# Slot sums and gathers of the first experts one item sooner, two decayed keys on GpSimd, the decay flag moved

## The chip, the cores and the metric

The kernel runs on one core of a Trainium2 chip. Four engines compute, each with its own program and in its own order: TensorE (PE in the profile, with its weight loads as PEld), VectorE (DVE), ScalarE (ACT) and GpSimd (POOL). SyncE (SP) issues transfers, and so do ACT and POOL. [...] The metric is the time of one execution on the device in microseconds (us); lower is better.

## The reference

Two stages in float32. The first is a linear attention with a decaying state, for 4 batches, 8 heads, 768 tokens and 48 values a head. The second sends each token to one of 8 experts, a network of two layers (384 to 1024 to 384). A token takes the expert of its largest logit, or, where its local gate is at least 0.5, the expert of the token before it.

```python
for t in range(S):
    kt, vt, rt = k[:, :, t], v[:, :, t], r[:, :, t]
    cur = einsum('bhd,bhe->bhde', u * kt, vt)
    y[:, :, t] = einsum('bhd,bhde->bhe', rt, state + cur)
    state = w * state + einsum('bhd,bhe->bhde', kt, vt)
...
fresh_e = argmax(logits[b, s])
e = fresh_e if s == 0 or local_gate[b, s] < 0.5 else prev_e
h = maximum(x[b, s] @ w1[e], 0.0)
out[b, s] = softmax(logits[b, s])[e] * (h @ w2[e])
```

## The kernel before

**Attention.** The work is cut into 16 items, numbered n: a batch and a pair of heads each. An item's 768 tokens are 6 chunks of 128. `scale` makes three products on POOL: `rw` (r times powers of the decay w), `ke` (k for the state) and `pd` (r times k, for a token's own term). `keys` makes `kw`, k times the inverse powers `inv`, on DVE. On PE, `scores` multiplies `kw` by `rw` into a bank called `pair`; DVE masks it into `am`. `own` multiplies `pd` into `y`, and DVE multiplies `y` by v. `added` sums k and v into the states' steps, DVE scans them into `S` (`states`), and `inside` and `before` add `am` and `S` to `y`. ACT copies `y` out as `xT`, `turn` transposes it, and a finished batch goes to memory as `x_d`. `run` interleaves the items by hand: in round n it does the scores of item n+1, the own terms of item n, and `inside` and `before` of item n-1. Item 15 is last; its two halves are copied as `xT` by ACT and as `end` by DVE (L318, L319).

**Routing.** The tokens are routed in two groups of two batches. For group 0 the steps lie between the rounds from n = 9 on (`g` is 8): experts, runs, counts, ranks, `slots` (a token's place in its expert's table), `columns` and `numbers` (tiles `eqv`, `val`), `places`, `apart` and `same` (the one-hot tile `ohq`). Then `summed` multiplies `val` by `ohq` on PE (L846), ACT copies the sums (`rows`), PE transposes them, and `head` turns them into token numbers (`gid`) on DVE. With these, `gather` has POOL fetch the rows of `x_d` (L1107, tile `xg`) for two early units of 168 tokens, units 0 and 1 (experts 0 and 1 with group 0's tokens). In rounds 14 to 16 `piece` brings unit 0's weights in four parts of 768 KB by SP; a one-element copy into each part holds it back until ACT comes by.

**Experts.** Behind the last item come the gate logits of the last batch (`logits`, 8 matmuls in two groups of four heads; a transpose of their result `lT`; a sum on DVE), the transposes of `xg` and their copies `exT`. Unit 0 then runs over eight blocks m of the hidden width: `hidden` (L1134), and one block behind it `output` (L1221). After block m of unit 0 comes step s = m of `routing`, and after block m of unit 1 step s = 8 + m: the same routing again for group 1. Step 4 holds a long run of small operations on DVE, from `exc` to `order` (L761 to L790). Units 0 and 1 are followed by 8 larger blocks, with matmul savings of Strassen's kind (`eleven`, `seven`).

**The decay flag.** `flag(0)` counts on DVE how many of w's values lie in the range for which the kernel is valid (tile `some`, four operations). `flag(1)` sums that over the partitions with a matmul of `some` and a column of ones on PE (L1698), then DVE makes `over` and `rare` of it. They stand in steps 13 and 14. The matmul writes one of two banks, `tp`, that the transposes of `xg` use in turn. Engines take their work strictly in the order in which this code is written.

Of the kernel before, what the change touches and what calls it, by code (L numbers as in the profile page):

```python
# [20 lines left out]
P = 128  # L21
# [31 lines left out]
VB = NCH * 2 * DH  # L53

# [7 lines left out]
class Attention:  # L62
# [140 lines left out]
    def scale(self, n):  # L203
# [28 lines left out]
    def keys(self, n):  # L232
        nc, t = self.nc, self.items[n]
        t["kw"] = self.two.tile([P, NCH, P], F32, name="kw")
        inv = self.inv[:, t["hp"]]
        for z in (slice(0, NCH),) if n > 2 else (slice(0, C2), slice(C2, NCH)):
            nc.vector.tensor_mul(t["kw"][:, z], t["kT"][:, z], spread(inv, 1, z.stop - z.start))
            if n < 3:
                self.decayed(nc.vector, n, z)
# [18 lines left out]
    def own(self, n, part=None):  # L258
# [3 lines left out]
        if part != 1:  # L262
            t["yy"] = y = None if last else self.py.tile([P, 2, 512], F32, name="y")
            t["y"] = [self.banks("yl")[:, 0] if last else y[:, h] for h in range(2)]
        for p in range(2):
            for h in range(2 if part != 1 else 0):
# [5 lines left out]
        if part == 0:  # L272
            return
# [30 lines left out]
    def before(self, n):  # L304
# [5 lines left out]
        for c, h in [(c, h) for h in range(2) for c in range(1, NCH)] if last else [(c, h) for c in range(1, NCH) for h in range(2)]:  # L310
# [44 lines left out]
    def run(self, router, fetch, heads):  # L355
# [11 lines left out]
        for n in range(M + 1):  # L367
# [37 lines left out]
            if n < M:  # L405
                self.turn(n - 2, pair("tp"))
                if n >= M - 2:
                    fetch(2 * (n - M + 2))
# [4 lines left out]
                if n > 3:  # L413
                    if n not in (g + 3, g + 5):
                        self.added(n)
# [12 lines left out]
            if n + 1 < M:  # L428
                self.scale(n + 1)
            if n == g + 6:  # L430
                router.numbers(0, self.nc.gpsimd)
# [7 lines left out]
            if n == g + 6:  # L439
                router.same(0, 1)  # L440
            if M - 2 <= n < M:
                fetch(2 * (n - M + 2) + 1)
            if n == 6:
                router.cast()
            if n == M:
# [20 lines left out]
            if ahead < M:  # L466
                self.scores(ahead, 0)()
# [1310 lines left out]
```

## Time and profile before

| | |
|---|---|
| three runs | 377.18, 378.99, 380.16 us |
| median | 378.99 us |
| the profiled execution's own time | 379.17 us |
| its span (first to last instruction) | 377.5 us |
| granted TensorE clock, mean over the span | 0.996 |
| chain that ended last | one POOL transfer of 0.97 us, 0.3% of the span |

The span is what the trace covers; the rest of the execution's time lies around it. The profiled execution is 0.18 us above the median. Its chain of waits is cut short behind the last transfer, so it says nothing of what bounds the kernel; that has to be read from the waits of PE and from the order of its work in time. In the rows, numbers after an engine's name are a line of the kernel, and a bracket at the end says how long the engine had stood idle and what released it.

### The profile page before, as it was taken

To read this page: it belongs to the slowest core of one execution; us is meant where nothing else is said; L and a number is where in the kernel's file an instruction comes from. 1 tells how busy PE (TensorE), PEld (TensorE's weight loads), DVE (VectorE), ACT (ScalarE), POOL (GpSimd) and SP (SyncE) were. 2 spreads that over 40 slices of the span, in tenths; PEclk is the share of its full clock that TensorE was granted. 3 is DMA by queue.
4 is the path that set the end of the run, shared out by engine and by line. 5 is a ranking of instruction groups with operands and counts; after the bars stand their busy time and mean duration, and the time that the engine had idled before them with its cause. 6 is when DMAs were issued, how large, how long until landed. Compare 5 with 4: busy or idle time off the path is not lost. (4 is left out here: it accounts for less than half of the span.)

```text
span 377.5 us, 9676 instructions
## 1 busy us (share of the span) xinstructions
PE 363.0 (96%) x3844; PEld 319.6 (85%) x3844; DVE 247.7 (66%) x718; ACT 110.3 (29%) x304; POOL 148.7 (39%) x207
## 2 busy tenths in 40 slices
PE   7899999999989999999999999999999999999992
PEld 6676777786769998999899999999999998989971
DVE  6988778888834835787557656857767767555300
ACT  4132233233532211322332233333243233331210
POOL 7689999786222055212333113313233023021012
PEclk9999999999999999999999999999999999999998
DMA  7999999983669457713352452164165065162011
GB/s 245 417 411 410 407 405 338 370 300 109 196 232 340 160 188 296 299 27 115 140 198 62 147 214 87 49 218 190 38 207 213 22 215 206 21 257 112 2 41 38
DMA packets 17765, 74.93 MB, mean 199 GB/s; under 512 B 2778, under 2 KB 6624, under 8 KB 15408
## 3 DMA queue, kind: packets, MB, share of 16 engines
q1 hardware_dynamic: 10336, 56.89, 40.7%
q0 software_dynamic: 3424, 9.48, 7.4%
q10 hardware_dynamic: 3952, 7.87, 5.7%
q8 instruction: 32, 0.52, 0.6%
q14 instruction: 21, 0.17, 0.1%
HBM read 64.79 MB, written 9.47 MB: 197 GB/s over the span
## 5 line engine op out<-in xcount | busy, mean ns | idle before, releaser
L1333 POOL DMA_INDIRECT out_dram<-yo,sid x27 | 26.6, 985 | 115.5 <-ACT yo L1328 92.0
L1184 PE MATMUL h<-exT,w1t 128*128 128x168 f32 (+4 forms) x240 | 54.9, 327 | 0.0
L1188 DVE TENSOR_TENSOR hT<-h,hs 128x168 f32<-128x168 f32 (+3 forms) x60 | 21.1, 351 | 46.1 <-PE h L1184 29.6
L1107 POOL DMA_INDIRECT xg<-x_d,gid x29 | 31.1, 1072 | 34.1 <-DVE gid L877 15.1
L1184 PEld LDWEIGHTS h<-exT,w1t 128*128 128x128 f32 x240 | 41.6, 190 | 0.3 <-issue 0.3
L1134 PE MATMUL h<-exT,w1t 128*128 128x168 f32 (+2 forms) x192 | 37.2, 333 | 0.5 <-DVE lt L698 0.5
L1253 PE MATMUL y<-factors,sums 128*128 128x192 f32 x168 | 36.8, 326 | 0.0
L293 DVE TENSOR_TENSOR am<-pair,kept 128x768 f32<-128x768 f32 x32 | 30.0, 953 | 8.9 <-PE pair L291 8.4
L217 POOL TENSOR_TENSOR pd<-rk 128x384 f32<-128x384 f32 x32 | 31.5, 1006 | 10.6 <-PE y L268 10.0
L1184 PE MATMUL h<-xs,ws 128*128 128x168 f32 (+4 forms) x144 | 35.3, 327 | 0.0
L1134 PEld LDWEIGHTS h<-exT,w1t 128*128 128x128 f32 x192 | 30.9, 190 | 2.6 <-DVE lt L698 0.6
L1184 PEld LDWEIGHTS h<-xs,ws 128*128 128x128 f32 x144 | 25.5, 190 | 4.3 <-ACT hs L1191 1.2
L1253 PEld LDWEIGHTS y<-factors,sums 128*128 128x128 f32 x168 | 28.9, 190 | 0.2
L291 PE MATMUL pair<-rw,kw 48*64 48x128 f32 (+1 forms) x768 | 23.4, 249 | 1.9 <-issue 1.1
L300 PE MATMUL y<-am,kv 128*64 128x128 f32 x360 | 22.9, 276 | 1.3 <-DVE y L276 1.2
L230 POOL TENSOR_TENSOR rw<-rk,tab 128x384 f32<-128x384 f32 x26 | 23.7, 936 | 0.4 <-DMA rk<-in_rk_dram 0.4
L1121 DVE COPY exT<-tp 128x384 f32<-128x384 f32 (+5 forms) x29 | 13.9, 485 | 14.7 <-PE tp L1120 14.6
L291 PEld LDWEIGHTS pair<-rw,kw 48*64 48x64 f32 x768 | 19.6, 133 | 4.6 <-issue 2.8
L1253 PE MATMUL y<-w2t,hT 128*128 128x192 f32 x96 | 23.0, 328 | 0.0
L213 POOL TENSOR_TENSOR ke<-kv,endT 128x288 f32<-128x288 f32 (+1 forms) x32 | 21.9, 705 | 1.9 <-DMA kv<-in_kv_dram 1.0
L321 ACT COPY xT<-y 128x768 f32<-128x768 f32 x15 | 12.0, 800 | 33.1 <-PE y L313 31.1
L300 PEld LDWEIGHTS y<-am,kv 128*64 128x64 f32 x360 | 19.4, 137 | 2.4 <-DVE y L276 1.7
(298 smaller groups left out, 736.6 us busy)
## 6 DMA issues: line engine op xcount, KB each, us to landing
w1t<-in_w_dram SPq DMA_DIRECT2D x8, 1536.0 KB, 6.9
w2t<-in_w_dram SPq DMA_DIRECT2D x8, 1536.0 KB
rk<-in_rk_dram SPq DMA_DIRECT2D x15, 768.0 KB, 8.4
kv<-in_kv_dram SPq DMA_DIRECT2D x16, 584.0 KB, 7.1
vT<-in_vT_dram SPq DMA_DIRECT2D x16, 384.0 KB
x_d<-x ACTq DMA_DIRECT2D x4, 1152.0 KB
w1t<-in_w_dram SPq DMA_DIRECT2D x2, 768.0 KB
w2t<-in_w_dram SPq DMA_DIRECT2D x2, 768.0 KB
```

The lines of the kernel that those rows point to most:

```text
L213: nc.gpsimd.tensor_mul(t["ke"][:, z], t["k"][:, z], spread(self.endT[:, p, hp], 1, len(range(NCH)[z])))
L217: nc.gpsimd.tensor_mul(t["pd"][:, z], t["rT"][:, z], t["kT"][:, z])
L230: engine.tensor_mul(t["rw"][:, z], t["rT"][:, z], spread(pw, 1, z.stop - z.start))
L291: nc.tensor.matmul(sc[f * DP:(f + 1) * DP, h, i, x:], lhsT=t["kw"][q, c, o * DP:(o + 1) * DP], rhs=t["rw"][q, c, x:], start=True, stop=True)
L293: return lambda: nc.vector.tensor_mul(t["am"][:, g], sc, spread(self.kept[:, g:g + 3], 1, 2))
L300: nc.tensor.matmul(t["y"][h][p * DP:(p + 1) * DP, c2 * P:(c2 + 1) * P], lhsT=t["v"][:, (2 * c + h) * DH:(2 * c + h) * DH + DP], rhs=t["am" ...
L1107: self.nc.gpsimd.indirect_dma_start(out=xg[:n], out_offset=None, in_=self.x_d[:rows], in_offset=bass.IndirectOffsetOnAxis(ap=u["gid"][:n, ...
L1134: nc.tensor.matmul(h[:, :n], lhsT=u["w1"][:, m, kk, :], rhs=u["xT"][:, kk, :], start=(kk == 0), stop=(kk == DK - 1))
L1184: nc.tensor.matmul(out, lhsT=a, rhs=b, start=start and k == 0, stop=stop and k == len(terms) - 1, skip_group_check=True)
L1188: nc.vector.tensor_tensor(out, a, b, op=Alu.add)
L1253: return lambda: nc.tensor.matmul(bank[:, x * half:(x + 1) * half], lhsT=a, rhs=b, start=(j == 0 and x == 0), stop=(j == FK // 2 - 1), ski ...
L1333: self.nc.gpsimd.indirect_dma_start(out=out.rearrange("n (h d) -> (n h) d", h=2) if half else out, out_offset=bass.IndirectOffsetOnAxis(ap ...
```

## The change

Its parts:

- For items 14 and 15 (`LATE`) `kw` is made on POOL instead of DVE, in two halves, between `ke` and `pd`. Since POOL takes its factor from SBUF, ACT copies two heads' pairs of `inv` to a tile `held` in round 6.
- Routing of group 0: `columns`, `places` (now two quarters on DVE) and `same` stand earlier, `numbers` stands ahead of `pd` of item 15, and `summed` moves from between the own terms of item 15 to the end of round 14. `head` and `gather` move to the start of round 15, behind `turn(13)`.
- The fourth part of unit 0's weights is held back by POOL until the rows of the second gather have landed.
- `before` of item 15 takes its two heads in turn, as with the other items, and no longer one after the other.
- Behind the last logits both tiles of `xg` are transposed first, then `lT`, then the last item; ACT copies the second tile, and also one tile of unit 2 in block 5 of unit 1.
- The decay flag moves from steps 13 and 14 to steps 5 and 6, and its matmul now takes `some` as a weight that is repeated over 128 columns.

```diff
-    def scale(self, n):
+    def scale(self, n, ahead=None):
...
         for what in (pd, ke) if n < 3 else (ke, rw, pd) if n == 4 else (rw, ke, pd):
+            if n in LATE and what is pd:
+                self.keys(n, nc.gpsimd)
+                if ahead:
+                    ahead()
             for i in range(2):
                 what(i)
...
-        for c, h in [(c, h) for h in range(2) for c in range(1, NCH)] if last else [(c, h) for c in range(1, NCH) for h in range(2)]:
+        for c, h in [(c, h) for c in range(1, NCH) for h in range(2)]:
...
                 self.turn(n - 2, pair("tp"))
+                if n == g + 6:
+                    router.same(0, 1)
+                if n == g + 7:
+                    router.head(self.pairs[0][:, 1, C2 * P:])
+                    heads()
...
+                self.held = self.late.tile([P, len(LATE), P], F32, name="held")
+                self.nc.scalar.copy(self.held, self.inv[:, HP - len(LATE):])
...
-                self.own(n, 0)
-                router.summed(0, 0)
-                self.own(n, 1)
-                router.copied(0)
+                self.own(n)
                 spare = self.py.tile([P, 2, 512], F32, name="y")
                 self.turn(n - 1, [spare[:, 0], spare[:, 1]])
-                router.head(self.pairs[0][:, 1])
-                heads()
...
             if n == g + 6:
-                router.places(0, 0)
+                self.added(n + 1)
+                router.summed(0, 0)
+                router.copied(0)
...
-        nc.scalar.copy(t[0:1, z.start, 0:1], self.ident[0:1, 0:1])
+        if k == 3:
+            nc.gpsimd.tensor_copy(t[0:1, z.start, 0:1], u["xg"][-1][0:1, 0:1])
+        else:
+            nc.scalar.copy(t[0:1, z.start, 0:1], self.ident[0:1, 0:1])
...
+        if s == 5:
+            self.flag(0)
         if s == 6:
+            self.flag(1, bank("fp"))
             self.fetch(EARLY, self.nc.sync, 1)
...
-        if s == 13:
-            self.flag(0)
-        if s == 14:
-            self.flag(1, bank("fp"))
...
+        for j in range(len(self.units[0]["rows"])):
+            self.turn(0, j, self.nc.scalar.copy if j else None)
+        att.token_logits(B - 1, yb[0])
         att.turn(B * HP - 1, yb[1:])
-        self.turn(0, 0)
-        att.token_logits(B - 1, yb[0])
-        self.turn(0, 1)
...
-                nc.tensor.matmul(fp[:1, :1], lhsT=some, rhs=router.ones[:, 0:1], start=True, stop=True)
+                nc.tensor.matmul(fp[:, :1], lhsT=some.to_broadcast([P, P]), rhs=router.ones[:, 0:1], start=True, stop=True)
```

In the lists that follow, a row is one or more instructions of one engine in program order, with the line of its own version of the kernel, the operation, the tile written and the tiles read.

POOL, items 14 and 15, before: `pd` of item 15 is followed by `val`, and that by the gathers of unit 0.

```order
L213 TENSOR_TENSOR ke<-kv_169,endT 128x3x96
L213 TENSOR_TENSOR ke<-kv_169,endT 128x2x96
L217 TENSOR_TENSOR pd<-rk_159 128x384 x2
L230 TENSOR_TENSOR rw<-rk_160,tab 128x384 x2
L213 TENSOR_TENSOR ke<-kv_165,endT 128x3x96
L213 TENSOR_TENSOR ke<-kv_165,endT 128x2x96
L217 TENSOR_TENSOR pd<-rk_160 128x384 x2
L818 TENSOR_TENSOR val_117<-eqv_116,t_527 128x384
L1107 DMA xg<-x_d,gid_95 128x384
L1107 DMA xg<-x_d,gid_95 40x384
```

The same place on POOL now.

```order
L214 TENSOR_TENSOR ke<-kv_169,endT 128x3x96
L214 TENSOR_TENSOR ke<-kv_169,endT 128x2x96
L245 TENSOR_TENSOR kw<-rk_159,held 128x384 x2
L218 TENSOR_TENSOR pd<-rk_159 128x384 x2
L235 TENSOR_TENSOR rw<-rk_160,tab 128x384 x2
L214 TENSOR_TENSOR ke<-kv_165,endT 128x3x96
L214 TENSOR_TENSOR ke<-kv_165,endT 128x2x96
L245 TENSOR_TENSOR kw<-rk_160,held 128x384 x2
L827 TENSOR_TENSOR val_117<-eqv_116,t_527 128x384
L218 TENSOR_TENSOR pd<-rk_160 128x384 x2
L1118 DMA xg<-x_d,gid_95 128x384
L1118 DMA xg<-x_d,gid_95 40x384
```

Two `kw` have come in ahead of the two `pd`, and `val` has gone ahead of the last one.

PE, from the last item's states to unit 0's first matmul, before (`lT` are the transposed logits, `end` the last head's output, `h` the hidden layer).

```order
L313 MATMUL pair_152<-rw,S 48x128 x5
L313 MATMUL pair_151<-rw,S 48x128 x5
L345 MATMUL y_1963<-xT,wp 32x384 x7
L345 MATMUL y_1963<-end_1895,wp 32x384
L332 MATMUL y_1964<-ident,xT 128x112 x3
L332 MATMUL y_1965<-ident,end_1895 128x112 x3
L1120 MATMUL tp_1938<-ident,xg 128x128 x3
L351 MATMUL y_1963<-ident,lT 128x128 x3
L1120 MATMUL tp_1937<-ident,xg 128x40 x3
L1134 MATMUL h<-exT,w1t 128x168 x6
```

The same place on PE now, from the last of the states' matmuls on.

```order
L318 MATMUL pair_152<-rw,S 48x128
L318 MATMUL pair_151<-rw,S 48x128
L350 MATMUL y_1968<-xT,wp 32x384 x7
L350 MATMUL y_1968<-end_1900,wp 32x384
L1131 MATMUL tp_1943<-ident,xg 128x128 x3
L1131 MATMUL tp_1942<-ident,xg 128x40 x3
L356 MATMUL y_1968<-ident,lT 128x128 x3
L337 MATMUL y_1969<-ident,xT 128x112 x3
L337 MATMUL y_1970<-ident,end_1900 128x112 x3
L1145 MATMUL h<-exT,w1t 128x168 x6
```

The states' matmuls alternate between the two banks, and the transposes of `xg` stand ahead of those of `lT` and of the last item.

PE behind block 6's hidden layer of unit 0, before.

```order
L1134 MATMUL h<-exT,w1t 128x168 x3
L1221 MATMUL y_2027<-hT,w2t 128x168
L1221 MATMUL y_2028<-hT,w2t 128x168
L1221 MATMUL y_2029<-hT,w2t 128x168
L1120 MATMUL tp_1937<-ident,xg 128x128 x3
L1134 MATMUL h<-exT,w1t 128x168 x3
```

The same place on PE now.

```order
L1145 MATMUL h<-exT,w1t 128x168 x3
L1232 MATMUL y_2032<-hT,w2t 128x168
L1232 MATMUL y_2033<-hT,w2t 128x168
L1232 MATMUL y_2034<-hT,w2t 128x168
L1708 MATMUL tp_1942<-r_ones,some 128x1
L1131 MATMUL tp_1943<-ident,xg 128x128 x3
```

The flag's matmul has come in ahead of the transposes of unit 1's first tile.

DVE at the end of step 4, before (`order` is the order of the blocks).

```order
L788 TENSOR_TENSOR num<-of,ief 1x64
L789 TENSOR_REDUCE orderf<-num 1x8
L790 CAST order<-orderf 1x8
L1121 COPY exT<-tp_1937 128x3x128
L1121 COPY exT<-tp_1938 128x3x40
```

The same place on DVE now.

```order
L797 TENSOR_TENSOR num<-of,ief 1x64
L798 TENSOR_REDUCE orderf<-num 1x8
L799 CAST order<-orderf 1x8
L1703 TENSOR_SCALAR ok<-w_t 128x4
L1704 TENSOR_SCALAR ok<-w_t 128x4
L1705 TENSOR_TENSOR ok<-ok 128x4
L1706 TENSOR_REDUCE some<-ok 128x1
L1709 TENSOR_SCALAR over<-tp_1942 1x1
L1710 CAST rare<-over 1x1
L1132 COPY exT<-tp_1943 128x3x128
```

The flag's six operations have come in between the last one of step 4 and the copies of unit 1's tiles.

More of the change, by code (lines that the diff above doesn't have):

```diff
@@ L1111, in gather, with turn @@
             u["xg"].append(xg)
-    def turn(self, i, j):
+    def turn(self, i, j, copy=None):
         nc, u = self.nc, self.units[i]
@@ L1568, in run @@
                 if m >= FK - after and not (following and m == FK - 1):
-                    self.turn(i + 1, m - (FK - after))
+                    self.turn(i + 1, m - (FK - after), self.nc.scalar.copy if following and m == FK - 3 else None)
             if i + 1 == EARLY:
@@ L1682 @@
         att = Attention(tc, st, rk_d, kv_d, vT_d, x_d, w_t, wp_d, kept, ident, lt, router.mp)
-        att.run(router, ex.piece, lambda: ex.gather(0))
+        att.run(router, ex.piece, lambda: (ex.gather(0), ex.piece(3)))
         ex.open(st)
```

52 lines of the change are left out of this document (26 added, 26 removed).

## The prediction

> **What bounds the kernel now.** I read the page's busy times first, then the waits of PE, then PE's program in time around the places that the change touches, and then DVE and POOL at the same times. From the page:
>
> ```profile
> PE 363.0 (96%) x3844; PEld 319.6 (85%) x3844; DVE 247.7 (66%) x718; ACT 110.3 (29%) x304; POOL 148.7 (39%) x207
> ```
>
> PE has work in 363.0 of 377.5 us. Of the 14.5 us left, some 7.4 lie behind its last matmul (370.04, below) and 1.6 ahead of its first (the first row of the next list). So whatever the change can win lies in a few short stalls, or in matmuls that run closer together, and whatever it adds to PE's waits lengthens the run. The waits of PE alone, by who was waited for:
>
> ```profile
> PE pair L151 <- POOL ident masks.py:199: 1.6, 1, 1.6
> PE tp L1120 <- DVE over L1699: 0.7, 1, 0.7
> PE tp L1120 <- DMA xg<-x_d,gid: 0.6, 1, 0.6
> PE h L1134 <- DVE lt L698: 0.5, 1, 0.5
> ```
>
> The other three are what the change is about: the flag, the first gather, and the copies ahead of unit 0's first matmul. Together they are under 2 us, 0.5% of the run. Here is PE's program between the last item and unit 0, in order of time (start, length, matmul records, and idle time before them):
>
> ```profile
> 106.93 1.20 PE L313 MATMUL pair<-rw,S 48*48 48x128 f32 x20
> 108.06 1.49 PE L345 MATMUL y<-xT,wp 128*32 128x384 f32 x14
> 109.23 0.83 PE L345 MATMUL y<-end,wp 128*32 128x384 f32 x2
> 109.99 0.51 PE L332 MATMUL y<-ident,xT 112*128 112x112 f32 x3
> 111.34 0.55 PE L1120 MATMUL tp<-ident,xg 128*128 128x128 f32 x3 [0.56 <-DMA xg<-x_d,gid]
> 111.73 0.49 PE L351 MATMUL y<-ident,lT 128*128 128x128 f32 x3
> 112.15 0.37 PE L1120 MATMUL tp<-ident,xg 40*128 40x40 f32 x3
> 113.02 1.98 PE L1134 MATMUL h<-exT,w1t 128*128 128x168 f32 x12 [0.50 <-DVE lt L698]
> ```
>
> From 106.93 to 113.02 are 6.09 us. The same steps in rounds where nothing waits, and the copy that the last logits wait for:
>
> ```profile
> 97.09 0.79 PE L313 MATMUL y<-rw,S 48*48 48x128 f32 x18
> 97.62 0.28 PE L291 MATMUL pair<-rw,kw 48*64 48x128 f32 x2
> 87.77 1.50 PE L345 MATMUL pair<-xT,wp 128*32 128x384 f32 x16
> 89.20 0.79 PE L332 MATMUL pair<-ident,xT 112*128 112x112 f32 x6
> 108.62 0.56 DVE L319 COPY end<-pair 128x384 f32<-128x384 f32 x1 [2.30 <-PE pair L313]
> ```
>
> **Between the last item and unit 0: 1.8 us gained.** An item that takes its two heads in turn has its states' matmuls through in 97.62 - 97.09 = 0.53, a little more with the two records that lie past it, say 0.63; item 15, one head after the other, takes 108.06 - 106.93 = 1.13. The new order makes it an item like the others: 0.5 gained. Eight logits without a wait take 89.20 - 87.77 = 1.43; here they take 109.99 - 108.06 = 1.93, because the last one starts at 109.23, behind the copy that ends at 109.18. In the new order that copy can still only start when the states are through, but the first four heads' logits (half of 1.43) cover its 0.56 nearly whole: some 0.4 gained. The two stalls of 0.56 and 0.50 are the third part. The gather is issued earlier (next paragraph), so the first should go. For the second, the transposes of `lT` and of the last item now stand between those of `xg` and unit 0; they take about 0.4 and 0.8 and cover both copies, with the short one on ACT behind `lT`. Sum 0.5 + 0.4 + 0.56 + 0.50 = 1.96; I take a gain of 1.8, nearer the upper end, since three of the four parts are read straight from rows and only the cover of the copies is argued. Bounds: 1.06 (the stalls alone) and 2.0. Late next is nothing on PE; ACT comes to the last item's copies and the store of `x_d` about 1 us later against unit 0, but the first gather that reads it starts at 132.88 (row below).
>
> **The sooner sums, and `kw` on POOL: 0.** The matmuls of `summed` stand at 103.84 and move to behind `added`, near 100.2; POOL's first gather starts at 106.45 and would start near 102.9.
>
> ```profile
> 100.42 0.66 PE L249 MATMUL mp<-kv,ke 128*48 128x48 f32 x20
> 103.84 0.86 PE L846 MATMUL mp<-ohq,val 128*32 128x128 f32 x24
> 84.42 1.35 POOL L213 TENSOR_TENSOR ke<-kv,endT 128x288 f32<-128x288 f32 x2
> 88.75 1.76 POOL L230 TENSOR_TENSOR rw<-rk,tab 128x384 f32<-128x384 f32 x2
> 94.66 1.98 POOL L217 TENSOR_TENSOR pd<-rk 128x384 f32<-128x384 f32 x2 [2.85 <-PE y L268]
> 106.45 1.27 POOL L1107 DMA_INDIRECT xg<-x_d,gid  x1 [7.72 <-DVE ex L919]
> 132.88 1.07 POOL L1107 DMA_INDIRECT xg<-x_d,gid  x1 [15.10 <-DVE gid L877]
> 92.33 0.28 PE L291 MATMUL pair<-rw,kw 48*64 48x128 f32 x2
> ```
>
> The first rows arrived 111.34 - 106.45 = 4.9 after the issue; the same from 102.9 gives 107.8, and PE wants them at 109.99 less the 0.9 gained ahead of them, 109.1. The tile `kw` is a product with a repeated factor like `rw`, so 1.8 to 2.0 for both halves. POOL ends `ke` of item 14 at 85.77 and makes `kw` by 87.8; PE's scores want it at 92.33. Then `pd`, `rw` and `ke` of item 15 run to about 92.8, `kw` of item 15 to 94.8, and its scores come at 97.62 (row above). POOL was idle for 2.85 ahead of the last `pd`, and the own terms that read it come at about 104. So POOL's 4 extra us lie beside other work with 2.8 us to spare, and DVE's 1.9 us of relief help nobody, since no wait above names `kw`. If POOL were slower by half, the cover would still hold. The one copy of `held` on ACT (0.4 to 0.5), the ACT copies of `exT`, and the fourth weight part, which is now held until about 108 and read by PE near 121, I cost at nothing for the same kind of reason: ACT is busy 29% of the time, and no PE wait above names it there.
>
> **The old flag: 0.85 gained.** The flag's matmul stands where the `xg` transposes need its bank:
>
> ```profile
> 142.63 0.19 PE L1698 MATMUL tp<-r_ones,some 128*1 128x1 f32 x2
> 143.50 0.87 PE L1120 MATMUL tp<-ident,xg 128*128 128x128 f32 x6 [0.69 <-DVE over L1699]
> ```
>
> From 142.63 to 143.50 are 0.87, matmul and stall together; without them 0.85 is saved (bounds 0.69 and 0.87).
>
> **The new flag: 3.9 lost.** Its matmul now stands on PE just ahead of the transposes at 125.38, and what it waits for, `some`, is made on DVE behind the whole of step 4:
>
> ```profile
> 124.52 1.02 PE L1221 MATMUL y<-hT,w2t 128*128 128x168 f32 x6
> 125.38 0.49 PE L1120 MATMUL tp<-ident,xg 128*128 128x128 f32 x3
> 122.18 0.37 DVE L761 TENSOR_TENSOR_SCAN exc<-seg,ext 128x104 f32<-128x104 f32 x1 [1.31 <-ACT ext L760]
> 128.35 0.16 DVE L790 CAST order<-orderf 1x8 int32<-1x8 f32 x1
> 128.43 0.73 DVE L1121 COPY exT<-tp 128x384 f32<-128x384 f32 x2
> 140.90 0.16 DVE L1693 TENSOR_SCALAR ok<-w_t 128x4 f32<-128x4 f32 x1
> 141.36 0.16 DVE L1696 TENSOR_REDUCE some<-ok 128x1 f32<-128x4 f32 x1
> 122.18:128.51 6.33, 6.33 (x66) 5.95 (x64) 5.81 (x19) 1.00 (x4) 0.00 (x0) 1.00 0.50 192
> ```
>
> The last row is a stretch: PE busy 6.33 of it, PEld 5.95, DVE 5.81 in 19 operations. DVE works through step 4 from 122.18 to 128.51 almost without a gap; it starts when the counts of the same step leave PE, so the block moves with PE and stays as late against it. Before the change the `exT` copies simply queued behind it and PE had other matmuls. Now the four operations of `flag(0)` follow at 128.43 and take 141.52 - 140.90 = 0.62: `some` is there at 129.05. PE loads it as a weight and runs the matmul (0.19), and is at the transposes at about 129.3 instead of 125.38: 3.9 lost. Behind the waiting matmul stand all of PE's later work, and with it the hidden layer, ACT and the next step of the routing; nothing of that can overtake. Bounds: 3.4, if DVE's gaps (6.33 - 5.81 = 0.5) closed, and 4.2 with slower hand-overs. No later stall of PE's list can take this up, since those left are under 1 us.
>
> **The sum.** -1.8 - 0.85 + 3.9 = +1.25 on the profiled execution's own 379.17, which gives 380.4; on the median of 378.99, which stands 0.18 lower, 380.2, and I say 380.3. With all bounds at one end: +0.5 (3.4 - 2.0 - 0.87) to +2.45 (4.2 - 1.06 - 0.69), so 379.5 to 381.4.
>
> **Rivals.** First, PE's clock falls in the new gap. What this trace shows of it is the end of the run (PE busy is the second number, its clock the third from the right):
>
> ```profile
> 367.64:370.05 2.41, 2.40 (x30) 1.84 (x26) 0.31 (x1) 0.00 (x0) 0.97 (x1) 1.00 0.16 57
> 371.10:374.40 3.30, 0.00 (x0) 0.00 (x0) 0.00 (x0) 0.00 (x0) 0.66 (x1) 1.00 0.15 36
> 374.50:377.40 2.90, 0.00 (x0) 0.00 (x0) 0.00 (x0) 0.00 (x0) 0.00 (x0) 0.50 0.03 8
> ```
>
> The last matmul ends at 370.04, the clock is still whole at 374.40 and half from 374.50: it took 4.4 us of idling, and the new gap is 3.6 to 3.9 (from 125.54, where the outputs end, or from 125.38). So by the row the clock stays. But one drop doesn't fix the point, and if the gap is enough in a run, the matmuls behind it run at half speed for a stretch, by my estimate about as long as the gap: half of 3.5, or 1.7, is lost, giving 382.0. If a second such stretch passes before the clock returns, 3.4 is lost, giving 383.7, slower by 1.2%; it decides from about 5 us at half clock on. [...] I give the first price 0.15 and the second 0.06.
>
> Second, the gap isn't there or is short, because `some` is ready near 125.4: then the change does what its flag edit can do at best, and the sum is -1.8 - 0.85, or 376.3. Against it stand DVE's order and the block of step 4 ahead of it. It would need the block to end 3 us sooner. 0.08.
>
> Third, POOL is late after all: `kw` for item 15 or the last `pd` misses its matmul, or the gather lands after 109.1. Each tenth of lateness beyond the 2.8 (or 1.3) spare shows one for one; I price it at the stalls that come back, 1.06, and half a us more, 380.3 + 1.06 + 0.5 = 381.9. POOL's rows of 1.7 to 2.0 for such pairs speak against it. 0.09.
>
> **How the numbers follow.** The forecast, a stall on the flag with the clock kept, has 0.62, with 379.5 to 381.4 as its own range. The three runs before spread over 377.2 to 380.2, 0.4% either way, so I widen: 378.7 at the low end. The high end, 382.9, takes in one stretch of half clock and a late POOL. A measurement of this kernel can tell about 1% from no change, 3.8 us: faster would need less than 375.2, below even the second rival, so 0.02. Slower needs over 382.8: the second price of the clock rival, and a tail of the others, 0.09. Within 1%: 0.89.
>
> **What would show it.** In the profile after: PE idle for about 3.6 us ahead of the one-column matmul of `some`, released by DVE, and no idle time ahead of the first `xg` transposes or unit 0's first matmul; the 20 states' matmuls of item 15 in about 0.6; from the first of them to unit 0 about 4.3 instead of 6.09; no PE wait on POOL's `kw`; the granted clock whole behind the gap. The forecast is wrong if that gap is under 2 us, or if the clock falls.

## The result, and the profile after

The changed kernel takes 387.08 us in the median of six runs (385.4 to 388.63), the kernel before 378.24 beside it (377.18 to 380.16). The ratio is 1.023, with a 95% interval of 1.020 to 1.025: 2.3% slower, where 380.3 was forecast with 382.9 as the upper end. The profiled execution is one of the quicker ones, 385.40 us with a span of 383.6, which is 6.23 above the profiled execution before. PE's busy time in the page after:

```profile
PE 364.2 (95%) x3844; PEld 320.5 (84%) x3844; DVE 246.5 (64%) x715; ACT 111.2 (29%) x306; POOL 152.5 (40%) x212
```

PE has as many matmuls as before and is busy 1.2 us longer, so some of them ran slower. The other 5 us are idle time. PE's waits after (who waited, for whom, us in total, times, longest) name it:

```profile
PE tp L1708 <- DVE some L1706: 3.5, 1, 3.5
PE tp L1131 <- DMA xg<-x_d,gid: 2.5, 1, 2.5
...
PE pair L864 <- ACT x L339: 0.8, 1, 0.8
...
PE y L1232 <- ACT hT L1148: 0.4, 1, 0.4
```

The first is the forecast gap. The second is a wait for the rows of unit 3, which the prediction didn't have at all; the 0.6 that the list before had under the same name were for unit 0's rows. The last two are small and new. PE's program in time around the last item (start, length, records, idle time before and its releaser):

```profile
101.59 0.33 PE L864 MATMUL pair<-ident,rows 128*128 128x128 f32 x1 [0.79 <-ACT x L339]
...
107.29 0.90 PE L318 MATMUL pair<-rw,S 48*48 48x128 f32 x20
...
111.39 1.89 PE L1145 MATMUL h<-exT,w1t 128*128 128x168 f32 x12
113.72 1.09 PE L1232 MATMUL y<-hT,w2t 128*128 128x168 f32 x6 [0.45 <-ACT hT L1148]
```

From 107.29 to 111.39 are 4.10 where there were 6.09, and neither the transposes of the gathered tiles nor unit 0's first matmul wait any more. But PE comes to 107.29 0.36 later than before (106.93), and unit 0's first output now waits. PE's program from unit 0's end to unit 3's first rows:

```profile
123.48 1.02 PE L1232 MATMUL y<-hT,w2t 128*128 128x168 f32 x6
128.03 0.38 PE L1708 MATMUL tp<-r_ones,some 128*128 128x1 f32 x2 [3.53 <-DVE some L1706]
128.28 0.53 PE L1131 MATMUL tp<-ident,xg 128*128 128x128 f32 x3
...
130.10 1.89 PE L1232 MATMUL y<-hT,w2t 128*128 128x168 f32 x6
...
133.16 1.12 PE L1232 MATMUL y<-hT,w2t 128*128 128x168 f32 x6
...
147.83 1.12 PE L1145 MATMUL h<-exT,w1t 128*128 128x168 f32 x6
...
157.75 0.55 PE L1131 MATMUL tp<-ident,xg 128*128 128x128 f32 x3 [2.47 <-DMA xg<-x_d,gid]
158.13 0.74 PE L1232 MATMUL y<-hT,w2t 128*128 128x168 f32 x4
```

Six outputs take 1.02 at 123.48 and 1.89 at 130.10. The stretches after say why; in each row the PEclk, third from the right, is the mean granted clock:

```profile
123.50:128.00 4.50, 1.00 (x8) 0.74 (x6) 4.17 (x15) 0.31 (x1) 0.00 (x0) 1.00 0.39 161
128.00:129.00 1.00, 0.97 (x8) 0.97 (x9) 0.45 (x3) 0.00 (x0) 0.00 (x0) 0.93 0.00 0
129.00:130.00 1.00, 1.00 (x5) 1.00 (x5) 0.39 (x1) 0.00 (x0) 0.00 (x0) 0.50 0.00 0
...
132.00:134.00 2.00, 2.00 (x33) 1.74 (x34) 0.28 (x1) 0.52 (x2) 0.00 (x0) 0.93 0.90 369
```

A mean of 0.93 over 128 to 129 puts the fall at 128.86 (0.14 us at half), and 0.93 over 132 to 134 the return at 132.27: 3.4 us at half clock, all of them with work. The same instruction in both programs, by its start, gives the account:

| PE instruction | before | after | after - before | what lies between |
|---|---|---|---|---|
| unit 0's first matmul | 113.02 | 111.39 | -1.63 | transition -1.99, 0.36 late into it |
| unit 0's first output | 114.83 | 113.72 | -1.11 | wait of 0.45 |
| unit 0's last but one output | 124.52 | 123.48 | -1.04 | |
| transposes behind the flag | 125.38 | 128.28 | +2.90 | the gap: +3.94 |
| second output behind the flag | 128.61 | 133.16 | +4.55 | half clock: +1.65 |
| unit 1's last hidden block | 144.30 | 147.83 | +3.53 | old flag: -1.02 |
| output behind unit 3's first rows | 151.92 | 158.13 | +6.21 | wait for rows: +2.68 |

After that nothing moves any more; the execution is 6.23 longer. Between these two executions, three terms made the difference to the forecast of +1.25: the clock, a gather that comes late, and -1.04 ahead of the flag where -1.8 was forecast.

Even the -1.04 is more than the change earned. In the profile before, PE stood still for 0.84 in the scores of item 13, which the change leaves as they are:

```profile
85.72 0.21 PE L291 MATMUL pair<-rw,kw 48*64 48x64 f32 x1 [0.84 <-issue]
```

The experiments below have three more profiles with the attention part as it was (flag_only, before_some_early, before_held). None of them has this wait, and they come to unit 0's last but one output at 123.20 to 123.31. Four more with the part as changed (flag_back, some_early, w1_held, filled_gap) come to it at 124.31 to 125.17. So the pair of the table sets a late execution of the old kernel against an early one of the new.

The median lies 1.7 above the profiled execution. Three of the six runs had a mean granted clock of 0.985 to 0.986, where the profiled one had 0.993. A stretch of 3.4 us at half lowers the mean over the run by 0.0044, and the half clock behind the last matmul, 3.0 us long in the profile before (374.47 to 377.5), counts in it too. The profile of flag_only (run 2) shows what 0.985 can be: 6.8 us at half inside the run and 4.5 at its end (380.00 to 384.5), against 3.4 and 2.15 in the changed kernel's. By this estimate the three runs had one stretch more, which is about the 1.7.

### The profile page after: what moved, and what is told of

Same layout as the page of the kernel before. It is cut to its first block, busy times and chain, and to the rows that moved or that the text cites. A ratio compares the mean times of both kernels' runs of the same rounds, so it can differ in the third digit from the quotient of the medians.

```text
span 383.6 us, 9679 instructions
## 1 busy us (share of the span) xinstructions
PE 364.2 (95%) x3844; PEld 320.5 (84%) x3844; DVE 246.5 (64%) x715; ACT 111.2 (29%) x306; POOL 152.5 (40%) x212
```

## The experiments

Theories. **Flag**: the flag's gap and what follows from it cost everything, and without it the rest of the change gains 1.8. **Attention**: the moved sums and gathers also cost something. **Clock**: a part of the loss is half clock behind the gap. **Overtaken gather**: the load of unit 3's first weights (`w1`, 1.5 MB) goes out before the issue of unit 3's first gather has ended, and its bytes delay the rows. **Keys**: `kw` on POOL costs. Each run has its own times of the kernel before, whose medians lie between 378.24 and 378.66; ratios are against those, with 95% intervals.

| kernel | median us | ratio [95%] | PE's wait for unit 3's rows, profiled | gap at the flag |
|---|---|---|---|---|
| changed kernel | 387.08 | 1.023 [1.020, 1.025] | 2.47 | 3.53 |
| 1 flag_back | 379.66 | 1.002 [0.999, 1.005] | 1.46 | none |
| 2 flag_only | 386.63 | 1.022 [1.016, 1.028] | 2.20 | 3.54 |
| 3 some_early | 383.28 | 1.013 [1.007, 1.018] | 2.52 | none |
| 4 before_some_early | 380.21 | 1.005 [1.002, 1.009] | 2.61 | none |
| 5 w1_held | 378.27 | 1.000 [0.997, 1.004] | none | none |
| 6 before_held | 377.35 | 0.998 [0.995, 1.000] | none | none |
| 7 filled_gap | 383.09 | 1.011 [1.007, 1.016] | 0.93 | filled |
| 8 kw_back | 381.07 | 1.007 [1.004, 1.010] | 0.89 | none |
| 9 held_kw_back | 378.50 | 1.000 [0.998, 1.002] | none | none |
| 10 third_first | 378.35 | 0.998 [0.995, 1.001] | none | none |
| 11 best | 377.81 | 0.998 [0.996, 1.000] | none | none |
| 12 best2 | 376.78 | 0.995 [0.994, 0.997] | none | none |
| 13 best2_pool_keys | 376.41 | 0.994 [0.992, 0.997] | none | none |

### 1. flag_back: the changed kernel with the flag in its old steps

```diff
         if s == 6:
-            self.flag(1, bank("fp"))
             self.fetch(EARLY, self.nc.sync, 1)
...
+        if s == 13:
+            self.flag(0)
+        if s == 14:
+            self.flag(1, bank("fp"))
```

(and `flag(0)` out of step 5.)

> The changed kernel with the decay flag back in steps 13 and 14; all else of the change stays. Theory F (the flag): the 3.5 us gap, the half clock behind it and the 2.5 us wait for unit 3's first rows all hang on the flag's new place, so all three go and the old stall of 0.7 at the flag comes back: about 377.2 us, 1 below before. Rival A (the attention part): the wait for unit 3's rows comes from the work moved in rounds 13 to 15 and on POOL, so it stays: about 379.7 us with a wait of 2 to 3 us there.

Measured 379.66, 7.4 below the changed kernel and not distinguishable from the kernel before. PE's waits and the old flag's place in it:

```profile
PE tp L1131 <- DMA xg<-x_d,gid: 1.5, 1, 1.5
PE pair L337 <- DVE am L298: 1.4, 2, 1.1
```

```profile
142.62 0.28 PE L1709 MATMUL tp<-r_ones,some 128*128 128x1 f32 x2
142.76 0.85 PE L1131 MATMUL tp<-ident,xg 128*128 128x128 f32 x6
```

The gap and the half clock are gone. At the old place nothing waits any more either: the tile copy that DVE did at 142.89, ahead of the flag's operations, is now ACT's at 141.97, so the bank of the next transposes is free sooner. Yet the gain is not there: a wait for rows of 1.46 and smaller ones stand in its place. The time is the one that rival A gave (379.7) and not that of theory F (377.2), though A's reason for the wait, the attention part, is refuted by the next runs. The flag's move made most of the loss, and the rest of the change is no gain of 1.8.

### 2. flag_only: the kernel before with the flag moved, and nothing else

```diff
+        if s == 5:
+            self.flag(0)
         if s == 6:
+            self.flag(1, bank("fp"))
...
-        if s == 13:
-            self.flag(0)
-        if s == 14:
-            self.flag(1, bank("fp"))
```

> The kernel before with nothing changed but the flag's place (steps 5 and 6, as in the changed kernel). Theory F: gap of 3.5 us or more, one or two stretches of half clock (1.7 us each), a wait of 1.5 to 3 us for unit 3's rows, less 0.85: 384 to 387 us. Rival A: no wait for unit 3's rows, 381 to 383 us.

Measured 386.63, within the expected 384 to 387: as much as the whole change loses, without any of its other parts. PE's wait for the flag, and stretches of this kernel:

```profile
PE tp L1697 <- DVE some L1695: 3.5, 1, 3.5
PE tp L1120 <- DMA xg<-x_d,gid: 3.3, 2, 2.2
```

```profile
127.00:127.50 0.50, 0.00 (x0) 0.00 (x0) 0.43 (x5) 0.00 (x0) 0.00 (x0) 0.92 0.00 0
127.50:129.00 1.50, 1.20 (x6) 1.20 (x7) 0.50 (x4) 0.00 (x0) 0.00 (x0) 0.50 0.00 0
...
134.00:135.00 1.00, 1.00 (x8) 0.94 (x9) 0.28 (x1) 0.36 (x2) 0.00 (x0) 0.88 0.98 418
```

Here the clock fell at 127.42, still inside the gap (0.92 over half a us: 0.08 at half), and came back at 134.24: 6.8 us, twice the stretch of the changed kernel's profile, from a gap of the same 3.54. The second part of the loss is the wait of 2.20 for unit 3's rows, in a kernel whose gathers and sums were not touched.

### 3 and 4. some_early and before_some_early: the flag's DVE part in step 2, its matmul in step 6

Third: the changed kernel with `flag(0)` moved from step 5 to step 2. DVE makes `some` long before the matmul, so there is no gap. Fourth: the same in the kernel before, without any other part of the change.

```diff
         if s == 2:
+            self.flag(0)
             r.turn_runs(1, bank("rp1"))
...
-        if s == 5:
-            self.flag(0)
```

> The changed kernel with the four DVE operations of the flag in step 2 instead of 5, where DVE idles; its matmul stays in step 6. Theory F, with the second mechanism in it (the old flag's stall kept unit 3's weights behind unit 3's first gather; without the stall they overtake it): no gap, no half clock, no stall at the old place, but a wait of 1.5 to 3 us ahead of unit 3's first transposes: about 378.8 us. Rival B (the slow stretch made the gather late): no such wait: about 376.3 us.

> The kernel before with the flag's four DVE operations in step 2 and its matmul in step 6: nothing but the old flag's stall is taken away. Second mechanism: the stall of 0.7 to 0.9 goes and a wait of 1.5 to 3 us for unit 3's rows takes its place: about 379.7 us. Rival B: 377.4 us, a plain gain of 0.85.

Measured 383.28 and 380.21. No gap and no stall on any flag is left in either, and both are slower than the kernel before. The second is 0.5 above its expected 379.7, but the first lies 4.5 above its 378.8. What they have in common is the wait for unit 3's first rows, 2.52 and 2.61. Here stands the release of that wait. In the kernel before, and then after, the issue of unit 3's first gather on POOL and of unit 3's `w1` on SP (start, length of the issue):

```profile
144.32 1.03 POOL L1107 DMA_INDIRECT xg<-x_d,gid  x1 [0.91 <-issue]
```

```profile
145.46 0.33 SPq L1082 DMA_DIRECT2D w1t<-in_w_dram  x1
```

```profile
148.55 1.21 POOL L1118 DMA_INDIRECT xg<-x_d,gid  x1 [0.58 <-issue]
```

```profile
148.98 0.33 SPq L1090 DMA_DIRECT2D w1t<-in_w_dram  x1
```

Before, the load goes out 0.11 behind the end of the gather's issue (145.46 against 145.35). After, it goes out 0.78 ahead of it (148.98 against 149.76). SP's load waits for unit 1's last hidden block (147.83 + 1.12), POOL's gather for ACT's copy of an earlier block, and the old flag's stall of 0.87 lay between the two on PE. With the stall gone the load comes 0.9 sooner against the end of the gather's issue. Over the kernels with an unheld load, from the load's lead and PE's wait: before -0.11 and none, flag_back 0.42 and 1.46, after 0.78 and 2.47, some_early 0.78 and 2.52, before_some_early 0.91 and 2.61, flag_only 0.91 and 2.20. Two kernels with a lead of some 0.8 waited less (filled_gap 0.93, kw_back 0.89), so the lead is not all of it.

### 5 and 6. w1_held and before_held: the load of unit 3's first weights held behind its gathers

```diff
+    def held_fetch(self, i):
...
+        self.nc.gpsimd.tensor_copy(u["w1"][0:1, 0, 0, 0:1], self.ident[0:1, 0:1])
+        self.nc.sync.dma_start(out=u["w1"].rearrange("p m k f -> p (m k f)"), in_=u["from"][0])
...
             if i == EARLY:
-                self.fetch(i + 1, self.nc.sync)
+                self.held_fetch(i + 1)
```

The one-element copy stands on POOL behind the four gathers, and SP's load has to wait for it. Fifth: some_early with this. Sixth: before_some_early with it.

> The kernel of some_early with one more edit: the load of unit 3's first weights waits, by a one-element copy on POOL, until POOL has issued unit 3's four gathers. Theory O (overtaking): the wait of 2.5 us for unit 3's rows is time that the gather's packets spend beside 1.5 MB of weights issued 0.4 to 0.9 us ahead of them; it goes wholly, and with it the second place where the clock can fall: 5 us below some_early in the median, about 377.5 to 378.5. Rival P (POOL issues those gathers too late in any case, the weights do not matter): 383, as some_early.

> The kernel before with the flag's DVE operations in step 2, its matmul in step 6, and unit 3's first weights held behind its gathers; nothing of the attention part of the change. Theory O: the old stall of 0.85 goes and no wait takes its place: 377.5, ratio about 0.9977. If the attention part gains 1 or more in best2, this one stands 1 above best2 plus 0.4; a rival that says the attention part gains nothing puts both at the same time.

Measured 378.27 against 383.28, and 377.35 against 380.21. DMA issues of w1_held, and of the kernel after, with the median us from issue to landing; in each case one `w1` and unit 3's first gather:

```profile
w1t<-in_w_dram SPq DMA_DIRECT2D x1, 1536.0 KB, 6.6
```

```profile
xg<-x_d,gid POOLq DMA_INDIRECT x1, 5.1
```

```profile
w1t<-in_w_dram SPq DMA_DIRECT2D x1, 1536.0 KB, 9.3
xg<-x_d,gid POOLq DMA_INDIRECT x1, 9.2
```

The rows land 5.1 after the issue when the load is held and 9.2 beside it, about when the load itself is through. Unit 3's rows no longer hold PE, and the load, 5.6 us later, is still in time. This shows the overtaken gather as the cause of that wait, and prices it at 5.0 and 2.9 us of the median (4.8 and 2.7 against each run's own times of the kernel before). In the profiles the wait itself is 2.5 and 2.6. The median of some_early lies 2.3 above its profiled 380.96, and two of its four runs had a mean clock of 0.989, which a stretch of half clock behind this wait would explain; no profile of those two exists.

Both times are as expected. The two kernels differ in nothing but the rest of the change, above all the attention part, and the one without it is the faster by 0.9 (377.35, with runs from 376.30 to 379.47, against 378.27, from 377.23 to 381.37). The other pairs that differ in it alone point the same way: some_early is 3.1 above before_some_early, and the changed kernel 0.45 above flag_only, though one kernel of each has only four runs. So no pair shows a gain, and by the first the attention part, as it stands in the change, costs about a microsecond.

### 7. filled_gap: PE kept busy in the gap

The changed kernel with 16 matmuls of `ident` (two records each) into the flag's bank, ahead of the flag's matmul. Their result is overwritten.

```diff
         if s == 6:
-            self.flag(1, bank("fp"))
+            fp = bank("fp")
+            for k in range(16):
+                self.nc.tensor.matmul(fp[:, :P], lhsT=self.ident, rhs=self.ident, start=True, stop=True)
+            self.flag(1, fp)
```

> The changed kernel with 16 matmuls of the identity (3.5 us of work that is not used) on PE ahead of the flag's matmul, inside the gap; the wait for the flag stays as long. Theory C (idling halves the clock): no half clock behind the gap, the wait for unit 3's rows stays: 1.7 to 2.5 us below the changed kernel, about 385. Rival: the half clock has another cause, 387 as the changed kernel.

Measured 383.09, 4.0 below the changed kernel. PE's program here, and a stretch of it:

```profile
125.17 1.02 PE L1232 MATMUL y<-hT,w2t 128*128 128x168 f32 x6
126.03 3.73 PE L1425 MATMUL tp<-ident 128*128 128x128 f32 x32
129.74 0.38 PE L1711 MATMUL tp<-r_ones,some 128*128 128x1 f32 x2
...
133.24 0.98 PE L1232 MATMUL y<-hT,w2t 128*128 128x168 f32 x5
```

```profile
130.00:132.00 2.00, 2.00 (x17) 1.96 (x16) 0.84 (x3) 0.31 (x1) 0.00 (x0) 1.00 0.00 0
```

The clock stays whole, and in all four runs of it the mean is 0.994 to 0.997, as in w1_held and best, which have no gap (0.993 to 0.997). This execution came to unit 0's last but one output 1.7 later than the changed kernel's profile (125.17 against 123.48). From there to the second output behind the flag it takes 8.07 (to 133.24), where the changed kernel took 9.68 (to 133.16): 1.61 saved, which is the price of the half clock read above. The 1.5 us between the two profiled executions are then left to a shorter wait for unit 3's rows, 0.93 instead of 2.47. That wait was expected to stay; why it shrank, with a lead of the load of 0.78 as before, is open, and so is how the 4.0 between the medians, more than the expected 1.7 to 2.5, divide. Shown is that the idle gap makes the half clock; its size, 1.65 in one profile and nearly twice that in flag_only's, is read from the profiles, not from the difference of medians.

### 8 and 9. kw_back and held_kw_back: the keys on DVE again

```diff
-LATE = (B * HP - 2, B * HP - 1)
+LATE = (98, 99)
...
-            if n in LATE and what is pd:
-                self.keys(n, nc.gpsimd)
-                if ahead:
-                    ahead()
+            if what is pd and ahead:
+                ahead()
```

Eighth: flag_back with this. Ninth: w1_held with this.

> The kernel of flag_back with the two decayed keys back on DVE. Theory D (POOL's products slow DVE's small operations, 0.17 us each without POOL and 0.4 to 1.0 beside it): the wait of 1.06 us ahead of the transposes in round 13 goes and nothing takes its place: about 378.6, 1 below flag_back. Rival: POOL's keys cost nothing, as the prediction said: 379.7 or above, since DVE has 1.9 us more to do.

> w1_held with the two decayed keys back on DVE: kw_back without the wait for unit 3's rows laid over it. Theory D: the wait for am ahead of the transposes in round 13, between 0.1 and 1.06 in the runs so far, stays at 0.3 or less in every profile: 0.3 to 0.7 below w1_held, 377.6 to 378. Rival: POOL's keys are free and DVE's 1.9 us more cost as much as they save: 378.3 or above.

Measured 381.07 (flag_back 379.66) and 378.50 (w1_held 378.27). The keys on DVE are no gain, so theory D fails by its times. kw_back's runs spread from 379.2 to 383.9, and with the load unheld they can't settle a few tenths; held_kw_back, with it held, shows no cost of the keys on POOL (w1_held, which has them there, is 0.2 lower). The theory's sign in the profiles is there, though: with the keys on DVE the wait for `am` ahead of the transposes in round 13 stays under 0.3 in both, where flag_back had this:

```profile
94.33 0.79 PE L337 MATMUL pair<-ident,xT 112*128 112x112 f32 x6 [1.06 <-DVE am L298]
```

### 10 to 13. The other small waits, and a version faster than both

third_first is w1_held with the third part of unit 0's weights issued ahead of `head` and the gathers. In round 15 of the change the gathers come first in the code, and with them the fourth part, which waits for their rows; the third part stands behind it on SP. SP's issues of parts three and four before, and after:

```profile
101.32 3.23 SPq L1096 DMA_DIRECT2D w2t<-in_w_dram  x2
```

```profile
107.50 0.80 SPq L1107 DMA_DIRECT2D w2t<-in_w_dram  x2
```

Both parts go out 6 us later. The one issued second, which is the third part, goes out at 107.92 and lands 5.7 after that, near 113.6; unit 0's first output wants it at 113.27 and starts at 113.72, so it was a matter of tenths, and w1_held's profile names the part outright:

```profile
114.70 1.09 PE L1243 MATMUL y<-hT,w2t 128*128 128x168 f32 x6 [0.81 <-DMA w2t<-in_w_dram]
```

```diff
                 if n == g + 7:
+                    fetch(2)
                     router.head(self.pairs[0][:, 1, C2 * P:])
                     heads()
-                if n >= M - 2:
-                    fetch(2 * (n - M + 2))
+                if n == M - 2:
+                    fetch(0)
```

> w1_held with the third part of unit 0's weights issued ahead of the fourth on SP, as in the kernel before (the change put the gather, and with it the fourth part's load, ahead of the third part's in the code of round 15). Theory S (SP's order): the third part stood behind the fourth, which waits for the gather's rows; the wait of 0.6 to 0.8 ahead of unit 0's first output is the third part landing late, and goes: 0.6 to 0.8 below w1_held, about 377.5. Rival: that wait is ACT's or DVE's, as the profiles of two of the runs name it, and stays: 378.3.

Measured 378.35: no gain over w1_held's 378.27, where 377.5 was expected, though the wait at the first output is gone from the profile. That profile has a wait of 1.08 for `am` of round 13 instead, which w1_held's has at 0.3, so the run doesn't tell.

best is held_kw_back with three more edits: the sums' transposes go to the bank that ACT isn't just copying from, the exponentials of group 0's gates (`powers(0)`, on ACT) come in step 0 instead of ahead of unit 0, and the copy of `held`, which nothing reads there, is left out.

```diff
-                    router.head(self.pairs[0][:, 1, C2 * P:])
+                    router.head(self.pairs[1][:, 1, C2 * P:])
...
         if s == 0:
+            r.powers(0)
...
-        self.router.powers(0)
```

> w1_held with the decayed keys back on DVE, the transposed sums in the bank that ACT does not read, and the exponentials of group 0 behind the first hidden block's copy on ACT. By the theories above: 378.5 before, less 0.85 for the flag's stall and 1.6 to 2 between the last item and unit 0, no new wait: 375.7 to 376.3. By a rival that says the attention part of the change gains nothing: 377.7.

Measured 377.81, the time of the rival and not the 375.7 to 376.3. The wait at the transposes of `rows` is down from 0.79 to 0.26, the first output still waits 0.60. best2 is best with third_first's edit as well.

> The kernel of best with the third part of the weights ahead of the fourth. Theory S: 0.6 below best, 377.2, ratio to before about 0.997. Rival: 377.8, as best.

Measured 376.78, 1.03 below best, and with an interval of 0.994 to 0.997 faster than the kernel before. Here the third part's order is worth more than the wait of 0.60 that it took away; in third_first it was worth nothing. What both show is the wait: the eight profiles with the change's order have 0.45 to 0.85 ahead of that output, and the three with the third part first have none. best2_pool_keys is best2 with the keys on POOL, as in the change.

> The faster version of the last runs, with the keys of items 14 and 15 on GpSimd again, as in the change. Theory that GpSimd's keys are late or slow VectorE's small operations beside them on a path that counts: 0.3 to 0.8 above that version's 376.8, so 377.1 to 377.6, and a wait ahead of the transposes of round 13 or of the last scan that VectorE's keys did not show. Rival, that they lie in cover: 376.8, within 0.3.

Measured 376.41, the lowest median of all (0.992 to 0.997). PE's longest waits of this kernel:

```profile
PE pair L152 <- POOL ident masks.py:199: 1.6, 1, 1.6
PE y L305 <- DVE y L281: 1.2, 2, 0.8
PE pair L296 <- ACT end L168: 0.6, 1, 0.6
PE pair L337 <- DVE am L298: 0.5, 2, 0.3
```

The two that follow are of 0.4 and 0.3, and none for the flag, the gathers or the weights is left. No cost of the keys on POOL shows here. This is the change with its four faults mended: the flag's DVE part three steps sooner, unit 3's load behind its gathers, the third weight part ahead of the fourth, and the other bank (with the exponentials moved). Against before_held, which has only the first two, its attention part, so mended, gains 0.9 us by the medians and 1.4 by the ratios, half to three quarters of the 1.8 forecast. The intervals of the two ratios overlap, so that gain is likely and not settled; best2, measured beside before_held, stands 0.6 below it, between the 1.4 and the 0 that were expected for a gain and for none.

## Why the prediction was wrong

**The flag's gap was right.** "Its matmul now stands on PE just ahead of the transposes at 125.38 ... 3.9 lost": measured 3.94 at the transposes, of it 3.53 idle, released by DVE's `some`. That DVE works through step 4 as late against PE as before held to a tenth.

**The clock was the first failed step.** "So by the row the clock stays" rested on one interval, 4.4 us from the last matmul to the fall at the end of the run, set against a gap of 3.6. That comparison has two faults, and the runs show both. The delay isn't fixed: from the end of the last matmul to the fall were 4.4 us in the changed kernel (124.50 to 128.86), 3.2 in flag_only (124.26 to 127.42) and 5.2 at the end of the changed kernel's run (376.26 to 381.45):

```profile
379.00:381.40 2.40, 0.00 (x0) 0.00 (x0) 0.00 (x0) 0.00 (x0) 0.00 (x0) 1.00 0.05 12
381.50:383.50 2.00, 0.00 (x0) 0.00 (x0) 0.00 (x0) 0.00 (x0) 0.00 (x0) 0.50 0.00 0
```

And work that comes back doesn't stop it: in the changed kernel PE had been at work again for 0.8 us when the clock fell. The price of one stretch, 1.7 by estimate, was right (1.65); that a stretch lasts about as long as the gap was no more than that estimate, and the two profiles with the gap have 3.41 and 6.82 at half. The chance of 0.15 for one and 0.06 for two was not: no run shows it, and in both kernels with the gap the profiled execution had at least one, and three of the other five runs of the changed kernel a lower mean clock still (0.985 to 0.986 against 0.993). What sets the moment of the fall was not shown either, so the runs give this count and no more.

**The old flag was the second.** "without them 0.85 is saved" was right at its place (1.02 measured). But the prediction looked only through PE's list of stalls for what a saving or a loss might meet later, and what came was a stall that the list didn't have. The old stall had kept PE, and with it the load that waits for PE, behind POOL's gather. Without it the load goes first and PE waits 2.5 for the rows. Runs 4, 5 and 6 show it: in the kernel before, the flag's move without any gap costs 0.5% with the load free; with the load held it gains 0.2%, by an interval that just reaches no change. The prediction asked what a stall's end brings next on PE alone; it did not ask who else had been waiting with PE.

**The fourth weight part at nothing was the third, a small one.** It looked at the part's own reader ("read by PE near 121") and at ACT, not at what stands behind it on SP's queue. The third part does, and its reader comes 8 us sooner. The price was 0.45 in the profile; by the medians it was 1.03 between best and best2, and nothing between w1_held and third_first.

**The transition was right at its place, and the attention part as a whole gained nothing.** "about 4.3 instead of 6.09" measured 4.10, and the waits for the rows and the copies went as said; only the states' matmuls, at 0.83 (107.29 to 108.12), saved less than the 0.5 forecast. But 1.8 was counted as if PE came to the transition at the same time and left it without a new wait. PE comes to it later: the five profiles with the change's attention part have item 15's states at 107.29 to 108.58, the three of the old part without the stall of 0.84 at 105.52 to 106.28. One wait on the way is in every one of the five: the `rows` transposes of the sooner sums write a bank that ACT still copies from (0.79 idle at 101.59). Behind the transition the third part of the weights takes 0.45 to 0.85. So the -1.04 of the two profiles, a little under the lower bound of 1.06, was luck, and the medians have the part at +0.9. The rival "POOL is late after all" is not what happened: the first gather started at 102.83 (102.9 was forecast) and landed in time, and `kw` on POOL showed no cost in the medians that can tell (9 and 13).

**The sum.** Forecast -1.8 + 3.9 - 0.85 = +1.25; measured between the two profiles -1.04 + 3.94 - 1.02 + 1.65 + 2.68 = +6.21. Two terms that stood at nothing make 4.3 of the 5.0 difference. Of the two, the clock was a rival, priced by itself, and the gather was priced nowhere; 382.9 as the upper end left no place for both. What remains open is a part of the other runs, up to 3.2 above the profiled execution: one more stretch of half clock, 1.65, would explain 386.74 and 387.41 at a mean clock of 0.985 to 0.986, but not all of 388.63, and not 387.83 at 0.993. No profile of these runs exists.

## What to carry to other kernels

A stall on the critical engine also paces the loads that wait for that engine (here 0.87 at the old flag, and 0.89 to 2.61 for unit 3's rows without it): before taking it out, look which transfer will now go out sooner, and whether a small gather with a near reader is issued just then. A gap of about 3.5 us on TensorE should be priced with a stretch at half clock behind it (3.41 and 6.82 us in the two profiles with such a gap), even where the record of one execution shows a longer delay (4.4). Two profiled executions can differ by stalls that belong to neither kernel (0.84 here), so a term of a microsecond that is read from one pair needs a second pair that differs in that part alone. And a transfer that is held back can hold what stands behind it on its queue (the third weight part went out 6 us later), so the order of issues on SP is part of every edit that holds one.

## What the runs showed of the hardware

In the two profiles with the flag's gap the granted clock fell once at it, to 0.50: a gap of 3.53 led to 3.41 us at half (the changed kernel), one of 3.54 to 6.82 (flag_only). The waits of 2.47, 2.20 and 2.52 for unit 3's rows (the changed kernel, flag_only, some_early) brought no fall in these profiles; the clock is 1.00 in the stretches over them. From the end of PE's last matmul to the fall were 3.2 us in flag_only's gap, 4.4 in the changed kernel's and at the end of the run before, and 5.2 at the end of the changed kernel's run. What sets this delay, and the time at half, is open.

Unit 3's first gather of rows took 5.0 to 5.8 us from issue to landing in four of the kernels with the load of 1.5 MB held (before_held 5.0, w1_held 5.1, best2 5.5, best2_pool_keys 5.8), and 7.4 to 9.2 in the seven in which that load was issued 0.4 to 0.9 us ahead of the end of the gather's issue.

One of VectorE's small operations took 1.04 us beside GpSimd's products in three profiles, and 0.17 without them. Both kernels do the same step here, flag_back with POOL's `kw` beside it and kw_back without; DVE's third operation on `si` in each:

```profile
92.37 1.04 DVE L817 TENSOR_SCALAR si<-si 128x12 int32<-128x12 int32 x1
```

```profile
92.24 0.17 DVE L815 TENSOR_SCALAR si<-si 128x12 int32<-128x12 int32 x1
```

The 1.04 are about as long as one of the two halves of `kw`, which POOL works on from 92.38 for 1.96 in the former. What lengthens the operation was not shown. Where this operation took 1.04 (flag_back, some_early, third_first), PE waited 0.75 to 1.08 for the `am` right behind it; where it took 0.16 beside the same products (the changed kernel, w1_held), at most 0.3. In the medians of runs 9 and 13 no cost shows.
